# Fetching a GpSimd unit's blocks in the middle of the unit before it, and preparing chunks nine slots ahead, in a one-core RWKV-7 + FFN kernel

## The chip, the cores and the metric

One Trainium2 chip, one core of it. The metric is device time of one execution in microseconds (us). A result is the median of several executions. The kernel before took 1062.97 us (three runs, 1060.01 to 1065.29) when the prediction was made. For a program on one core the state of a run (fast or slow) is told from its distance to the fastest run of the same kernel.

## The reference

A recurrence over 768 steps for 4 batches and 8 heads of width 40, then a feed-forward block on its output. The kernel must give the (3072, 320) result.

```python
def _attn_ref(r, k, v, w, a, b):              # each (4, 8, 768, 40)
    for t in range(S):
        y[:, :, t] = einsum('bhd,bhde->bhe', r_t, state)
        Sa = einsum('bhde,bhe->bhd', state, a_t)
        state = state * w_t[:, :, None, :] - einsum('bhd,bhe->bhde', Sa, b_t) \
                + einsum('bhd,bhe->bhde', v_t, k_t)

x = y.transpose(0, 2, 1, 3).reshape(3072, 320)
h = maximum(x @ w_in, 0)                      # w_in (320, 2048)
out = (h * h) @ w_out                         # w_out (2048, 320)
```

## The kernel before

The sequence is cut into 24 chunks of 128 steps (6 for each of 4 batches). Within a chunk the recurrence becomes triangular systems of 64x64 blocks, two for each head. The work on a chunk has four parts: `prepare` makes the blocks N and stores them to HBM (`kept_d`, and decays to `kept_e`); GpSimd fetches them, solves the triangular systems, and stores the inverses (`kept_t`); `rest` loads the inverse T of the *next* chunk and makes its remaining operands; `chain` applies the chunk to the state. The feed-forward block (`second`) fills TensorE in between.

The loop goes over slots; slot i runs the chain of chunk i. GpSimd solves for several chunks at once, called a unit here: units 4 to 9 hold chunks 6-7, 8-9, 10-13, 14-17, 18-21 and 22-23. One unit must be stored before the next is fetched into the same tile `half_n`.

```python
def take(u, queues):                          # fetch the blocks of unit u
    ...
    for col in range(cols):
        queues[col % len(queues)].dma_start(out=part_of(u)[col * rows:(col + 1) * rows], in_=kept)

def solve(u, between={}):
    ...
    for s in range(size - 1):                 # 63 steps of two instructions
        if s in between:
            between[s]()
        ...
        nc.gpsimd.tensor_tensor(p_, part[...], t3[...], Alu.mult)
        nc.gpsimd.tensor_tensor(t3[...], t3[...], p_, Alu.subtract)
    ...
    nc.gpsimd.dma_start(out=to, in_=ts)       # the inverses, to kept_t
```

Apart from GpSimd's own fetches and stores and a few early transfers, loads and stores go through SyncE's one queue, in program order. A store is put off by a few steps; `flush` puts all that still wait into the queue. A load of a chunk's inputs:

```python
def load(i, g=None):
    x_ = loaded[i] = {"k": fetch("k", k, i)}
    if g is not None:
        ...
        nc.sync.dma_start(out=g["dec"][:USED], in_=kept_e[i])
    x_["r"] = fetch("r", r, i)
    later(lambda: x_.update(v=fetch("v", v, i), b=fetch("b", b, i)), ...)
```

And the loop. `ahead[i]` are the chunks prepared in slot i; `weave` interleaves the jobs of a slot; a unit is fetched and solved after the first slot that completes the preparation of its chunks.

```python
ahead = {0: (4, 5), 1: (6, 7), 2: (8,), 3: (9,), 4: (10, 11), 5: (12, 13)}
ahead.update({i: (i + 8,) for i in range(6, len(order) - 8)})
...
for i in range(len(order)):
    ...
    jobs = [(chain(i, g), 11, 0, TOTAL) if i else (first_slot, 10, 0, TOTAL)]
    jobs.append((some(second, n), n, begin, TOTAL))
    made = ahead.get(i, ())
    for j, m_ in enumerate(made):
        jobs.append((prepare(m_), 5, ...))
    done.update(made)
    if i + 1 < len(order):
        if i:
            ready[i + 1] = {}
            load(i + 1, ready[i + 1])
        jobs.append((rest(i + 1, ready[i + 1]), 9, 2, TOTAL))
    ...
    weave(*jobs)
    while unit < len(units) and all(m_ in done for m_ in ... if unit_of[m_] == unit):
        flush()
        take(unit, own)                       # own = [nc.gpsimd]
        solve(unit)
        unit += 1
```

## Time and profile before

| | before |
|---|---|
| median of 4 runs, beside the changed kernel | 1064.13 us (1060.01 to 1065.83) |
| span of the profiled execution | 1062.7 us |
| busy TensorE | 946.3 us (89%) |
| busy GpSimd | 667.7 us (63%) |
| mean granted TensorE clock | 0.900 |
| GpSimd's waits for stored blocks before a fetch | 36.3 us |

How to read it: the granted clock is the share of TensorE's full speed that it was allowed; half clock is 0.50. TensorE is the busiest engine, and slot 13 shows it full, with 0.3 us idle in 43.8 at clock 1.00; so a slot that is much longer than its like has either idle TensorE time or a clock below 1.00 in it. A line of SyncE's queue (SPq) tells when a transfer was issued and how long the issuing took, not when it landed. The token copies in it gather the recurrence's output for the feed-forward block. The lines themselves stand in the prediction.

### The profile page before, as it was taken

The page shows a single profiled execution, that of the slowest core. Times are in us where ns is not written, and L with a number is a line of the kernel's source. Part 1 is how long each engine was busy: PE and PEld are TensorE (multiplying, and loading weights), DVE is VectorE, ACT ScalarE, POOL GpSimd, SP SyncE. Part 2 cuts the span into 40 slices and gives each one's busy share as a digit, 9 for nine tenths or more (in the row PEclk, how much of TensorE's full clock was granted, in tenths as well). Part 3 has the DMA queues.
Part 4 walks back from the last instruction along what each step waited for, and adds up shares of the span by engine and source line. Part 5 has one row for each costly group of instructions (what it writes and reads, how often), then busy time and mean ns, then how long its engine had stood idle before and what let it go on. Part 6 is the DMA issues. An engine that isn't in the chain of part 4 may idle for free.

```text
span 1062.7 us, 19797 instructions
## 1 busy us (share of the span) xinstructions
PE 946.3 (89%) x7824; PEld 687.5 (65%) x7824; DVE 493.5 (46%) x940; ACT 273.3 (26%) x627; POOL 667.7 (63%) x1124
## 2 busy tenths in 40 slices
PE   6366667789999999997999998999997999999998
PEld 5255566576677766774677666776675677757656
DVE  5447786687463475442653453353522442222120
ACT  3132332343322223222212222213211222232020
POOL 4778464884888599981899951899968980000000
PEclk8656565568999999998999999899998999999999
DMA  8987989659457917447747618544345431430000
GB/s 109 149 142 141 183 185 184 138 123 195 87 90 127 196 32 115 89 64 171 113 60 135 112 55 148 91 97 77 50 112 95 65 48 53 97 46 7 22 1 19
DMA packets 260168, 106.92 MB, mean 101 GB/s; under 512 B 243660, under 2 KB 249292, under 8 KB 258412
## 3 DMA queue, kind: packets, MB, share of 16 engines
q1 hardware_dynamic: 255740, 86.65, 46.8%
q0 software_dynamic: 3248, 18.88, 7.7%
q8 instruction: 62, 1.02, 0.4%
q10 hardware_dynamic: 1088, 0.13, 0.1%
q14 instruction: 30, 0.25, 0.1%
HBM read 72.47 MB, written 31.19 MB: 98 GB/s over the span
## 4 chain that ended last, share of the span: by engine, by line
PE 60%; DMA 14%; POOL 13%; SPq 4%; DVE 3%; issue 3%; ACT 3%; POOLq 0%; ACTq 0%; DVEq 0%
PE ps_f L87 27%; PE ps_w L87 14%; PE ps_c L87 13%; POOL half_t L437 6%; POOL half_p L435 6%; DMA in_v<-in_v_dram 5%; PE ps_w L314 4%; SPq L108 2%; DMA in_k<-in_k_dram 2%; DMA half_n<-kept_d 1%; DMA tokens<-tokens 1%; DMA kept_t<-half_t 1%; DMA kept_e<-decay 1%; SPq L142 1%; PE ps_c L609 1%
## 5 line engine op out<-in xcount | busy, mean ns | idle before, releaser
L435 POOL TENSOR_TENSOR half_p<-half_n,half_t 128x70 f32<-128x70 f32 (+52 forms) x502 | 297.7, 593 | 111.3 <-DMA half_n<-kept_d 60.0
L437 POOL TENSOR_TENSOR half_t<-half_t,half_p 128x70 f32<-128x70 f32 (+52 forms) x502 | 322.6, 643 | 39.3
L87 PE MATMUL ps_f<-w_out,hid 128*128 128x320 f32 x672 | 202.0, 445 | 0.0
L87 PE MATMUL ps_f<-tokens,w_in 128*128 128x384 f32 x448 | 160.1, 500 | 0.0
L653 DVE TENSOR_TENSOR hid<-hid 128x384 f32<-128x384 f32 x128 | 91.8, 734 | 142.4 <-ACT hid L671 142.2
L87 PEld LDWEIGHTS ps_f<-w_out,hid 128*128 128x128 f32 x672 | 123.3, 193 | 46.7 <-issue 4.7
L87 PEld LDWEIGHTS ps_f<-tokens,w_in 128*128 128x128 f32 x448 | 80.8, 190 | 76.4 <-issue 32.1
L671 ACT ACTIVATE hid<-ps_f 128x384 f32<-128x384 f32 x112 | 54.9, 490 | 199.1 <-PE ps_f L87 199.1
L330 DVE TENSOR_TENSOR A<-ps_w,upper 128x512 f32<-128x512 f32 x48 | 30.9, 685 | 91.3 <-PE ps_w L87 91.3
L506 DVE TENSOR_TENSOR kvT<-ps_w,dec 128x512 f32<-128x512 f32 x24 | 16.5, 687 | 100.8 <-PE ps_w L314 60.8
L87 PE MATMUL ps_c<-xr,T 64*64 64x40 f32 x768 | 40.0, 245 | 21.3 <-DMA T<-kept_t 14.6
L87 PE MATMUL ps_f<-tokens,w_third 64*128 64x384 f32 x224 | 55.1, 540 | 0.0
L87 PEld LDWEIGHTS ps_c<-xr,T 64*64 64x64 f32 x768 | 33.3, 151 | 32.7 <-issue 16.0
L351 DVE TENSOR_TENSOR_SCAN decay<-ps_w,ones 128x64 f32<-128x64 f32 x88 | 23.6, 268 | 64.9 <-PE ps_w L314 64.8
L87 PE MATMUL ps_w<-decay,bT 40*128 40x128 f32 x352 | 30.9, 324 | 21.5 <-DVE decay L360 21.5
L87 PEld LDWEIGHTS ps_w<-decay,bT 40*128 40x128 f32 x352 | 26.1, 222 | 30.1 <-DVE decay L360 14.8
L330 DVE TENSOR_TENSOR RX<-ps_w,upper 128x512 f32<-128x512 f32 x48 | 30.8, 684 | 31.7 <-PE ps_w L87 31.5
L330 DVE TENSOR_TENSOR RV<-ps_w,upper 128x512 f32<-128x512 f32 x48 | 30.9, 685 | 21.9 <-PE ps_w L87 21.6
L87 PE MATMUL ps_w<-rT,xnT 40*128 40x128 f32 x384 | 37.1, 306 | 2.3 <-ACT rT L516 1.9
L355 DVE RECIPROCAL decay<-decay 128x256 f32<-128x256 f32 x22 | 38.3, 1740 | 0.0
L356 DVE RECIPROCAL decay<-decay 128x256 f32<-128x256 f32 x22 | 37.2, 1692 | 0.0
L87 PEld LDWEIGHTS ps_w<-rT,kvT 40*128 40x128 f32 x384 | 28.0, 209 | 13.2 <-issue 4.6
(139 smaller groups left out, 1401.7 us busy)
## 6 DMA issues: line engine op xcount, KB each, us to landing
kept_e<-decay SPq DMA_DIRECT2D x22, 633.8 KB
dec<-kept_e SPq DMA_DIRECT2D x22, 633.8 KB
hid<-in_moe_w_out_dram SPq DMA_DIRECT2D x16, 320.0 KB
half_n<-kept_d POOLq DMA_DIRECT2D x12, 384.0 KB, 11.2
half_n<-kept_d POOLq DMA_DIRECT2D x6, 768.0 KB, 12.0
in_w<-in_w_dram SPq DMA_DIRECT2D x24, 160.0 KB
in_ab<-in_b_dram SPq DMA_DIRECT2D x24, 160.0 KB
in_ab<-in_a_dram SPq DMA_DIRECT2D x24, 160.0 KB
```

What stands on the lines that cost most here:

```text
L87: nc.tensor.matmul(o, l_, r_, start=start, stop=True, skip_group_check=True)
L108: later(lambda: queue.dma_start(out=out_, in_=in_), steps)
L314: nc.tensor.transpose(p_[:, q * 128:(q + 1) * 128], pair(x_, q), ident)
L330: nc.vector.tensor_tensor(t_, p_, over4(upper), Alu.mult)
L351: nc.vector.tensor_tensor_scan(up[:, q, MID + 1:C + 1], wT[:, q, MID:], ones, 1.0, Alu.mult, Alu.mult)
L355: nc.vector.reciprocal(down[:, :, MID + 1:C + 1], up[:, :, MID + 1:C + 1])
L356: nc.vector.reciprocal(up[:, :, :MID], down[:, :, :MID])
L435: nc.gpsimd.tensor_tensor(p_, part[:, at:at + m_].unsqueeze(1).to_broadcast([128, n, m_]), t3[:, :n, s:s + 1].to_broadcast([128, n, m_]), ...
L437: nc.gpsimd.tensor_tensor(t3[:, :n, s + 1:], t3[:, :n, s + 1:], p_, Alu.subtract)
L506: nc.vector.tensor_tensor(kT, kT_, down[:, :, 1:C + 1], Alu.mult)
L653: nc.vector.tensor_tensor(h_, h_, h_, Alu.mult)
L671: nc.scalar.activation(h_, p_, Act.Relu)
```

## The change

The intent is to let GpSimd start its units earlier, so that T is there when TensorE comes to it. Four things are done. Unit 4 stops after 33 of its 63 steps to fetch the first two thirds of unit 5's blocks. To have these in time, chunks 8 and 9 are both prepared in slot 2. From slot 9 on preparation runs nine slots ahead, not eight (slot 9 prepares two chunks). And the two groups of small matmuls that join the halves of the fine units' inverses (units 0 to 3, which solve blocks of 32x32) alternate between the upper and lower partitions.

```diff
+    EARLIER = Q * HC
-    def take(u, queues):
+    def take(u, queues, words=slice(None)):
 ...
-            queues[col % len(queues)].dma_start(out=part_of(u)[col * rows:(col + 1) * rows], in_=kept)
+            queues[col % len(queues)].dma_start(out=part_of(u)[col * rows:(col + 1) * rows, words], in_=kept[:, words])
+    def solving(u, between={}, stop=None):      # solve(), as a generator
 ...
+            if s == stop:
+                yield
 ...
-        for one, two in ends_:
-            for h in range(H):
+        for h in range(H):
+            for one, two in ends_:
                 mm(p_[two, h], g["joins"][one, h], upper_[one, h], True)
 ... (the second group likewise)
-    ahead = {0: (4, 5), 1: (6, 7), 2: (8,), 3: (9,), 4: (10, 11), 5: (12, 13)}
-    ahead.update({i: (i + 8,) for i in range(6, len(order) - 8)})
+    ahead = {0: (4, 5), 1: (6, 7), 2: (8, 9), 3: (10,), 4: (11,), 5: (12, 13)}
+    ahead.update({i: (i + 8,) for i in range(6, 9)})
+    ahead[9] = (17, 18)
+    ahead.update({i: (i + 9,) for i in range(10, len(order) - 9)})
 ...
+    AHEAD, under_way = (FINE,), []              # FINE is 4
 ...
-            take(unit, own)
-            solve(unit)
+            if under_way:
+                take(unit, own, slice(0, EARLIER))
+                run(under_way.pop())
+                take(unit, own, slice(EARLIER, Q * (HC + Q)))
+            else:
+                take(unit, own)
+            if unit in AHEAD:
+                under_way.append(solving(unit, stop=Q + 1))
+                next(under_way[0])
+            else:
+                solve(unit)
```

More of the change, by code (lines that the diff above doesn't have):

```diff
@@ L411, in take @@
         for col in range(cols):
-            queues[col % len(queues)].dma_start(out=part_of(u)[col * rows:(col + 1) * rows], in_=kept)
+            queues[col % len(queues)].dma_start(out=part_of(u)[col * rows:(col + 1) * rows, words], in_=kept[:, words])
     def solve(u, between={}):
+        run(solving(u, between))
+    def solving(u, between={}, stop=None):
         first, nb = units[u]
@@ L483, in inverses @@
         p_ = small()
-        for one, two in ends_:
-            for h in range(H):
+        for h in range(H):
+            for one, two in ends_:
                 mm(p_[one, h], mv[two, h], blocks[two, h], True)
```

## The prediction

> **What bounds the kernel now.** I number the loop's steps as slots (slot i runs the chain of chunk i) and GpSimd's blocks of triangular solves as units: unit 4 solves chunks 6-7, unit 5 8-9, unit 6 10-13, unit 7 14-17, unit 8 18-21, unit 9 22-23. I read the page's slices first.
>
> ```profile
> PE   6366667789999999997999998999997999999998
> PEclk8656565568999999998999999899998999999999
> ```
>
> Until about slice 9 (some 240 us) TensorE is neither full nor at full clock: slots 0 to 3 run on latency and transfers. After that it is full, with dips. I then cut the span at slot starts (the matmuls into ps_c from A and in_v begin a slot): us, then busy us of PE, PEld, DVE, ACT, POOL, then granted clock, DMA share and GB/s. These are slots 1, 2, 4, 10, 13, 14, 18.
>
> ```profile
> 105.00:154.70 49.70, 33.06 (x332) 28.47 (x330) 38.02 (x69) 17.22 (x37) 28.05 (x80) 0.60 0.97 190
> 154.70:195.40 40.70, 31.31 (x293) 26.58 (x292) 26.83 (x57) 13.72 (x33) 21.98 (x49) 0.54 0.76 141
> 234.40:282.70 48.30, 45.35 (x410) 32.53 (x408) 34.47 (x73) 18.29 (x43) 31.99 (x75) 0.89 0.72 139
> 473.40:527.40 54.00, 45.50 (x342) 29.34 (x340) 23.20 (x43) 13.46 (x30) 27.47 (x47) 0.94 0.70 133
> 598.50:642.30 43.80, 43.48 (x342) 28.41 (x340) 21.33 (x44) 13.36 (x30) 27.02 (x38) 1.00 0.45 91
> 642.30:683.00 40.70, 37.31 (x316) 28.03 (x314) 14.17 (x30) 7.18 (x17) 20.56 (x35) 0.92 0.70 109
> 791.30:836.00 44.70, 37.18 (x297) 25.88 (x296) 11.98 (x22) 8.21 (x19) 32.83 (x62) 0.92 0.61 110
> ```
>
> Slot 13 is the healthy pattern: 0.3 us idle, clock 1.00. Slots 10, 14 and 18 lose idle time, and then clock: 6% of 54.0 = 3.2 us, 8% of 40.7 = 3.3, 8% of 44.7 = 3.6. TensorE's timeline says what each waits for.
>
> ```profile
> 487.09 1.08 PE L87 MATMUL ps_c<-xr,T 64*64 64x40 f32 x16 [7.07 <-DMA T<-kept_t]
> 663.76 0.63 PE L314 MATMUL ps_w<-ident,in_r 128*128 128x128 f32 x4 [2.88 <-DMA in_r<-in_r_dram]
> 803.75 1.08 PE L87 MATMUL ps_c<-xr,T 64*64 64x40 f32 x16 [7.52 <-DMA T<-kept_t]
> ```
>
> So TensorE's work is the bound from 240 us on, plus three interruptions. GpSimd's own timeline says where they come from (start, duration, then the wait before).
>
> ```profile
> 250.62 0.60 POOL L440 DMA_DIRECT2D kept_t<-half_t  x1 [0.30 <-POOL half_t L437]
> 255.83 0.96 POOL L425 MEMSET half_t<- 128x1024 f32 x1 [2.67 <-DMA kept_t<-half_t]
> 265.67 0.28 POOL L435 TENSOR_TENSOR half_p<-half_n,half_t 128x63 f32<-128x63 f32 x1 [8.23 <-DMA half_n<-kept_d]
> ...
> 479.40 0.60 POOL L440 DMA_DIRECT2D kept_t<-half_t  x1 [0.30 <-POOL half_t L437]
> 490.35 1.03 POOL L412 DMA_DIRECT2D half_n<-kept_d  x2 [10.35 <-DMA kept_d<-N]
> ...
> 647.25 1.03 POOL L412 DMA_DIRECT2D half_n<-kept_d  x2 [18.62 <-DMA kept_d<-N]
> ...
> 784.52 0.60 POOL L440 DMA_DIRECT2D kept_t<-half_t  x1 [0.30 <-POOL half_t L437]
> 798.76 0.29 POOL L435 TENSOR_TENSOR half_p<-half_n,half_t 128x63 f32<-128x63 f32 x1 [7.21 <-DMA half_n<-kept_d]
> ```
>
> The stall at 487 is unit 6 ending late (479.40): true GpSimd lateness. The one at 663 is unit 8's 1.5 MB fetch, issued at 647.25, burying the loads of slot 14. The one at 803 looks like GpSimd, but is not: unit 8 was stored at 784.5; the SyncE queue shows the load of T behind token copies, which lie under unit 9's fetch.
>
> ```profile
> 786.82 13.33 SPq L108 DMA_DIRECT2D tokens<-tokens  x8
> 800.25 1.37 SPq L451 DMA_DIRECT2D T<-kept_t  x2
> ```
>
> **What the Trainium skill says.** "DMA: Bandwidth & Descriptors", Queues, rings and completion order: each DMA engine takes turns between its queues, packet by packet. The trace agrees: half_n moves in 12 KB rows, T in 256 B rows, tokens in 1.5 KB rows, so small rows beside a fetch get a turn per big row, and the token copies ended (800.2) only as the fetch did (798.8). "TensorE: Matmul & The Clock Gate", What's actually happening: an idle window of about 3.4 us halves the clock. The trace agrees after both 7 us stalls (xr,T takes 1.08 us, 0.66 elsewhere); a wait of 2.88 + 0.43 us (in_r, in_v) was enough in slot 14. "TensorEngine Tiling (Array Packing)", Key Properties: different tiles can run in parallel. Only in part here: matmuls of 40x128 on alternating halves take 72 ns each (1.16 us / 16)[...], but the 64x40 ones, which alternate already, take 41 ns, no less than that rule gives (37).
>
> **The change, part by part.** (a) *Fetch within unit 4.* It stops after step 32 (about 214.8 us in the old trace) to issue four fetches of the first 2/3 of unit 5's words (4 x 0.49 = 2.0 us), and the last third after its end. Its end moves from 250.6 to 252.6. Unit 5 now waits only for unit 4's store (5.2 us, as 250.62 to 255.83) and two kinds of memset (1.6): it starts at 259.4 instead of 265.7, 6.3 us earlier. Needed: chunk 9's first blocks by 214.8. Both 8 and 9 are made in slot 2 now; slot 2, with two preparations, should grow from 41 towards slot 1's 50 us, ending about 202, and stores end some 8 to 12 us later: just in time, 0 to 3 us of wait possible. (b) *Units 5 and 6* then run 79.8 us, 12.5 of fetch and 121.3 us: unit 6 ends at 473.1, not 479.4. (c) *Slot 9 prepares 17 and 18*: 2.9 us of TensorE work (transposes 0.6 + 1.1, products 1.16) comes ahead of the first stall, so TensorE comes to chunk 10's T at about 483, not 480. Free of other traffic T would arrive 7.7 us after unit 6's end (as 479.40 to 487.09), at 480.8, and the stall would vanish. But the stores of chunk 17 now go into the SyncE queue *before* the load of T (they came behind it, which made unit 7 wait until 490.35). So unit 7's fetch leaves at once and meets T's load. By unit 9's case (784.52 to 798.76) it takes 14.2 us from a unit's end: 487.3, and T comes about 1 us after it, 488. Gain there: 2.9 us of work done early, less 0.9 of later T: 2.0 us, the clock loss staying. (d) *Unit 7* starts at 487.5 instead of 506.3, ends at 609.3 (121.8 us). Its fetch no longer falls on slot 10's in_r and in_v (1.2 us of stall), but they queue behind the late T: net 0 to 1. (e) *Nine ahead*: chunk 21 is made in slot 12, so unit 8 starts fetching at 609 rather than 647, in the middle of slot 13, when its loads are done. Slot 14's stall goes: 3.3 + 3.3 of clock = 6.6 us. Unit 8 ends at 609.3 + 14.2 + 121.2 = 744.7; unit 9's fetch then ends near 759, long before slot 17's token copies. They take about 6 us (188.25 to 194.6 in the same trace), T comes 7 us sooner: 7.5 + 3.6 of clock, less 0.5 left over, 10.6 us. (f) *Early slots*: slot 2 grows by some 7, slot 4 shrinks by some 4 to 6 (one preparation less). Unless TensorE comes to chunk 10 after 488, it hides in the wait for T. (g) *Joins*: 32 matmuls of 54 ns at half clock (34 at full), twice in each of six chunks. With 41 ns for those that alternate already I expect at most 0.3 us a group, under 2 us of busy time, in slots that wait for transfers: 0. Sum: 2.0 + 0.5 + 6.6 + 10.6 = 19.7, less 1 for a new collision around 745 to 760 (slot 17's loads of in_k and dec): 18.7. 1063 - 19 = **1044 us**.
>
> **Rivals.** (1) *T does not meet the fetch, or passes it.* Then the whole 7.07 goes with its 3.2 of clock, 6 to 9 us more: 1036. For: T is only 256 KB; against: the token copies at 787. (2) *Unit 4 waits in its middle for chunk 9.* Early DMA is nearly full (0.97 in slot 1) and half clock rules there; each us of that wait moves units 5, 6 and T: 1049 if 5 us. For: the estimate is just in time. (3) *The fetches only collide elsewhere*: unit 9's with slot 17, unit 5's 1 MB at 215 with slot 3. If slot 17 stalls as slot 14 did, 6.6 comes back: 1050. Against: slot 17's in_k was asked 7.5 us before its slot. (4) *The early slots grow beyond what the wait hides* (slot 2 past 52): 1 us for 1 us, 1050 to 1056.
>
> **Range and chances.** 1034 to 1055: rival 1 sets the low end, two of the others together the high one. 2% faster is 1041.7, just under my figure: faster 0.38, within 2% 0.59, slower 0.03. Most of the gain rests on two stalls whose cause is seen in the trace, hence little chance of slower.
>
> **What would show it.** Unit 5's first solve about 6 us earlier; half_n's waits for kept_d (36.3 us in all) below 12; unit 6's end at 471 to 476, T's matmul at 486 to 490 after a wait of 3 to 6; no waits of 2 us for in_r nor for T in slots 14 and 18; clock 1.00 there; busy PE nearly unchanged (946), its idle some 15 us less. Wrong would be: T on time at 481 (rival 1); unit 4's middle waiting over 4 us (2); a new TensorE wait of over 2 us in slots 15 to 17 (3); slot 5 starting over 8 us later (4).

## The result, and the profile after

The changed kernel took 1051.36 us (median of four runs, 1047.30 to 1053.37), the kernel before 1064.13 us in the same rounds: a ratio of 0.9881, 95% interval 0.9837 to 0.9925. Ratios here are always the mean time of one kernel's fast runs over the mean of the other's fast runs of the same rounds, so not quite the ratio of the quoted medians. The gain is 1.2%, 12.8 us by the medians: within 2%, and inside the range. It is less than the 19 us that the prediction's sum had.

The profiled execution of the changed kernel spans 1045.6 us. It is the fastest of the four runs (1047.30 us as timed), while the profiled execution of the kernel before (1064.37 us as timed) lies at its median; so part of the 17.1 us between the two profiles is the draw of the execution.

The page's slices of the changed kernel, to be held against the first two lines of the prediction:

```profile
PE   6364665688999999997999999999999999999998
PEclk8656676667999999998999999999999999999999
```

After slice 9 one dip is left where there were three. It is the one that the prediction said would stay, around 480 us. The same cut at slot starts, for slots 2, 10, 14, 15 and 18 of the changed kernel (us, busy us of PE, PEld, DVE, ACT, POOL, granted clock, DMA share, GB/s):

```profile
152.80:202.80 50.00, 31.24 (x323) 27.05 (x320) 32.46 (x69) 15.46 (x37) 29.70 (x61) 0.64 0.87 170
477.50:528.40 50.90, 45.22 (x344) 29.43 (x343) 26.40 (x43) 13.36 (x30) 38.80 (x49) 0.93 0.74 144
643.30:677.40 34.10, 33.78 (x316) 25.92 (x314) 15.79 (x30) 7.08 (x17) 31.67 (x32) 1.00 0.33 60
677.40:712.70 35.30, 33.83 (x296) 24.04 (x294) 11.92 (x20) 8.92 (x21) 33.02 (x30) 1.00 0.70 125
783.40:819.00 35.60, 35.06 (x299) 24.47 (x298) 12.10 (x22) 8.21 (x19) 31.92 (x48) 1.00 0.62 109
```

Slots 14 and 18 are healthy: 0.3 and 0.5 us idle, clock 1.00; they are 6.6 and 9.1 us shorter in this cut. Slot 10 still has 5.7 us of idle time and clock 0.93. TensorE's timeline shows the two waits that are left:

```profile
489.53 1.08 PE L87 MATMUL ps_c<-xr,T 64*64 64x40 f32 x16 [5.44 <-DMA T<-kept_t]
687.36 0.66 PE L314 MATMUL ps_w<-ident,in_k 128*128 128x128 f32 x4 [0.96 <-DMA in_k<-in_k_dram]
```

T at 489.53 came 2.4 us *later* than before (487.09), although GpSimd was earlier. The wait of 0.96 us for in_k in slot 15 is new. GpSimd's timeline of the changed kernel (start, duration, wait before):

```profile
213.44 2.00 POOL L415 DMA_DIRECT2D half_n<-kept_d  x4
258.15 0.29 POOL L443 TENSOR_TENSOR half_p<-half_n,half_t 128x63 f32<-128x63 f32 x1
488.18 0.28 POOL L443 TENSOR_TENSOR half_p<-half_n,half_t 128x63 f32<-128x63 f32 x1 [6.11 <-DMA half_n<-kept_d]
610.52 1.03 POOL L415 DMA_DIRECT2D half_n<-kept_d  x2 [0.16 <-DMA dec<-kept_e]
```

The fetch in the middle of unit 4 left at 213.44 without a wait, and unit 5 began to solve at 258.15, 7.5 us earlier than before. Unit 7 began at 488.18, and T was taken 1.35 us after that. Unit 8's fetch left at 610.52, not 647.25. GpSimd's waits for blocks that were not yet stored, from the view of waits (total us, times, longest), were 36.3 us before:

```profile
POOL half_n L415 <- DMA kept_d<-N: 7.3, 1, 7.3
```

SyncE's queue at the end of slot 17 and the start of slot 18 answers to the last two lines of the prediction's first part. The eight token copies took 6.32 us in place of 13.33, and the load of T went out in time:

```profile
778.88 6.32 SPq L108 DMA_DIRECT2D tokens<-tokens  x8
785.30 1.38 SPq L459 DMA_DIRECT2D T<-kept_t  x2
```

Where the 17.1 us of this pair of profiles lie: slot 10 ended 0.9 us later (528.35 against 527.45), slot 14 gave 6.5, slot 15 gave 2.4 (the preparation that slot 9 now does, less the new wait), slot 18 gave 9.2. That is 17.2.

### The profile page after: what moved, and what is told of

Its sections match the earlier page's. It is cut to its first block, busy times and chain, and to the rows that moved or that the text cites.

```text
span 1045.6 us, 19803 instructions
## 1 busy us (share of the span) xinstructions
PE 927.4 (89%) x7824; PEld 672.1 (64%) x7824; DVE 496.8 (48%) x940; ACT 273.0 (26%) x627; POOL 670.6 (64%) x1128
## 4 chain that ended last, share of the span: by engine, by line
PE 52%; POOL 28%; DMA 10%; issue 5%; DVE 2%; ACT 2%; SPq 1%; POOLq 0%; DVEq 0%; ACTq 0%
PE ps_f L87 26%; POOL half_t L445 14%; POOL half_p L443 13%; PE ps_w L87 11%; PE ps_c L87 10%; DMA half_n<-kept_d 3%; PE ps_w L314 2%; DMA kept_t<-half_t 1%; DMA half_n<-kept_q 1%; DMA in_w<-in_w_dram 1%; DMA T<-kept_t 1%; DMA w_out<-in_moe_w_in_dram 1%; PE ps_w L542 1%; DMA kept_m<-N 1%; POOL half_n L415 1%
## 5 line engine op out<-in xcount | busy, mean ns | idle before, releaser
L443 POOL TENSOR_TENSOR half_p<-half_n,half_t 128x70 f32<-128x70 f32 (+52 forms) x502 | 298.9, 595 | 90.2 <-DMA half_n<-kept_d 39.8
L87 PE MATMUL ps_f<-w_out,hid 128*128 128x320 f32 x672 | 198.6, 440 | 0.0
L87 PE MATMUL ps_f<-tokens,w_in 128*128 128x384 f32 x448 | 162.3, 506 | 0.0
L661 DVE TENSOR_TENSOR hid<-hid 128x384 f32<-128x384 f32 x128 | 94.4, 752 | 139.4 <-ACT hid L679 139.0
L87 PEld LDWEIGHTS ps_f<-w_out,hid 128*128 128x128 f32 x672 | 121.6, 190 | 44.9 <-issue 2.1
L514 DVE TENSOR_TENSOR kvT<-ps_w,dec 128x512 f32<-128x512 f32 x24 | 16.5, 687 | 88.7 <-DMA dec<-kept_e 46.6
L87 PE MATMUL ps_c<-xr,T 64*64 64x40 f32 x768 | 39.1, 242 | 13.7 <-ACT xr L592 6.7
L351 DVE TENSOR_TENSOR_SCAN decay<-ps_w,ones 128x64 f32<-128x64 f32 x88 | 23.8, 270 | 54.2 <-PE ps_w L314 54.1
L87 PEld LDWEIGHTS ps_c<-xr,T 64*64 64x64 f32 x768 | 32.5, 148 | 25.1 <-ACT xr L592 13.1
L87 PE MATMUL ps_w<-rT,xnT 40*128 40x128 f32 x384 | 34.2, 293 | 2.4 <-ACT rT L524 2.4
L524 ACT COPY rT<-ps_w 128x512 f32<-128x512 f32 x24 | 14.0, 585 | 82.5 <-PE ps_w L314 82.5
```

The lines of the kernel that those rows point to most:

```text
L87: nc.tensor.matmul(o, l_, r_, start=start, stop=True, skip_group_check=True)
L351: nc.vector.tensor_tensor_scan(up[:, q, MID + 1:C + 1], wT[:, q, MID:], ones, 1.0, Alu.mult, Alu.mult)
L443: nc.gpsimd.tensor_tensor(p_, part[:, at:at + m_].unsqueeze(1).to_broadcast([128, n, m_]), t3[:, :n, s:s + 1].to_broadcast([128, n, m_]), ...
L514: nc.vector.tensor_tensor(kT, kT_, down[:, :, 1:C + 1], Alu.mult)
L524: nc.scalar.copy(rT, turn(x_["r"]))
L661: nc.vector.tensor_tensor(h_, h_, h_, Alu.mult)
```

## The experiments

Twelve kernels ran (one of them the changed kernel again), all gave correct results, in three batches of four. Each batch was on one chip and shared its runs of the kernel before (medians 1065.53, 1063.97, 1063.76 us). Slot lengths are from each kernel's one profile.

| kernel | median us | ratio to before (95%) | slot 10 | slot 14 | slot 15 | slot 18 |
|---|---|---|---|---|---|---|
| before | 1064.13 | 1 | 54.1 | 40.6 | 37.7 | 44.7 |
| changed | 1051.36 | 0.9881 (.9837-.9925) | 50.9 | 34.1 | 35.3 | 35.6 |
| *batch 1:* after_again | 1050.90 | 0.9858 (.9831-.9886) | 49.8 | 34.4 | 39.8 | 35.7 |
| t_first | 1053.68 | 0.9886 (.9863-.9908) | 57.5 | 34.1 | 35.1 | 35.6 |
| no_mid_fetch | 1053.39 | 0.9889 (.9867-.9911) | 53.0 | 34.1 | 35.2 | 35.6 |
| no_nine | 1063.89 | 0.9988 (.9963-1.0013) | 50.3 | 41.1 | 37.4 | 44.9 |
| *batch 2:* k_first | 1049.10 | 0.9851 (.9828-.9874) | 53.2 | 34.3 | 34.5 | 35.6 |
| t_k_first | 1041.37 | 0.9789 (.9770-.9809) | 43.8 | 34.1 | 34.5 | 35.6 |
| r_first | 1041.91 | 0.9785 (.9765-.9805) | 44.9 | 34.1 | 34.5 | 35.6 |
| only_nine | 1051.43 | 0.9885 (.9864-.9906) | 52.8 | 34.1 | 35.4 | 35.6 |
| *batch 3:* before_late9 | 1063.73 | 1.0007 (.9981-1.0033) | 49.9 | 40.3 | 37.4 | 40.1 |
| old_joins | 1050.17 | 0.9875 (.9850-.9899) | 49.9 | 34.4 | 37.0 | 35.9 |
| t_k_no_mid | 1043.73 | 0.9814 (.9790-.9837) | 45.0 | 34.1 | 34.5 | 35.6 |
| nine_late | 1068.81 | 1.0059 (1.0027-1.0091) | 72.6 | 34.1 | 35.7 | 35.7 |

The theory under test: nearly all of the gain is the nine-ahead order, which takes big fetches off the loads of slots 14 and 18; in slot 10 the earlier GpSimd is worth little because unit 7's fetch now meets the load of T. The rivals: the mid-unit fetch carries the gain; GpSimd is simply still late in slot 10; the joins matter.

### after_again: the changed kernel, unchanged

> The changed kernel unaltered, a second time: how far its executions spread, and whether its profile is the same in the places that count. Theory (mine, from the two profiles): slot 10 waits 5 to 6 us for the T of chunk 10, slots 14 and 18 wait for nothing; 1047 to 1054 us. Rival: the profile of the changed kernel was a lucky execution (it is the fastest of four), and others show a further wait of 3 us or more, which explains why the median gain is 12 us where the profile's is 17.

Measured: 1050.90 us, ratio 0.9858, profiled span 1051.5 us. This profile is nearer the median than the first one, and it shows a loss that the first did not. The first line is slot 15 of it from the cut by windows, the second its start of work on in_k:

```profile
678.70:718.50 39.80, 36.86 (x294) 25.86 (x292) 12.53 (x20) 8.92 (x21) 37.21 (x34) 0.91 0.63 111
```

```profile
690.12 1.11 PE L314 MATMUL ps_w<-ident,in_k 128*128 128x128 f32 x4 [2.43 <-DMA in_k<-in_k_dram]
```

The wait for in_k was 2.43 us here, and the matmuls after it ran at half clock (1.11 us for what took 0.66); the slot lost 4.5 us against the first profile. SyncE's queue shows why the wait exists at all. First the kernel before, whose slot 15 began at 682.95; then this one, whose slot 15 began at 678.66:

```profile
685.34 0.40 SPq L142 DMA_DIRECT2D in_k<-in_k_dram  x1
...
688.77 3.57 SPq L108 DMA_DIRECT2D kept_d<-N  x4
```

```profile
680.04 4.49 SPq L108 DMA_DIRECT2D kept_d<-N  x4
...
685.28 0.56 SPq L142 DMA_DIRECT2D in_k<-in_k_dram  x1
```

Before, the load of in_k went out 2.4 us into the slot, ahead of the stores of prepared blocks; now these stores come first and it goes out 6.6 us into the slot. What follows: the changed kernel has one new wait, in slot 15, which cost about 1 us in one profile and about 5 in the other (39.8 us against the 34.5 that the slot takes without it, in k_first below). Both profiles have the same order in the queue; what differs is how long the load took to land after its issue (3.3 and 4.8 us) and the clock after it. Seven kept profiles have this order: in five of them slot 15 took 35.1 to 35.7 us, in old_joins 37.0 and here 39.8, so the dear case is seen in two of seven. The expectation missed in slot 10: TensorE waited 3.02 us for T, not 5 to 6. It came 1.8 us later to it than in the first profile, T came 0.7 earlier, and the slot ended at 529.01 (528.35 there).

### no_nine and only_nine: the order of preparation, taken out and alone

no_nine is the changed kernel with `ahead` from slot 6 on as before:

```diff
-    ahead.update({i: (i + 8,) for i in range(6, 9)})
-    ahead[9] = (17, 18)
-    ahead.update({i: (i + 9,) for i in range(10, len(order) - 9)})
+    ahead.update({i: (i + 8,) for i in range(6, len(order) - 8)})
```

> The changed kernel with the old look-ahead of eight slots from slot 9 on. Theory: the stores of chunk 17 come again behind the load of T, unit 7's fetch leaves after T has landed, T comes at about 483, the wait in slot 10 shrinks to 1 to 2 us without half clock; but unit 8's fetch falls on slot 14's loads again (6 to 7 us lost there) and unit 9's on the token copies before slot 18 (3 to 8 us lost). Sum: 3 to 8 us over the changed kernel, 4 to 10 under the kernel before. Rival (nine ahead does nothing but fill slot 10): slots 14 and 18 without waits.

only_nine is the kernel before with these lines alone:

```diff
-    ahead.update({i: (i + 8,) for i in range(6, len(order) - 8)})
+    ahead.update({i: (i + 8,) for i in range(6, 9)})
+    ahead[9] = (17, 18)
+    ahead.update({i: (i + 9,) for i in range(10, len(order) - 9)})
```

> The kernel before with the nine slots ahead from slot 9 on, and nothing else of the change. Theory: early slots as before (4 us shorter than in the changed kernel); unit 6 ends at 479 to 480, unit 7's fetch leaves at once, T comes with its end at about 494, TensorE comes there at 483: about 10 us of wait. Slots 14 and 18 lose nothing. 2 to 6 us over the changed kernel, 1053 to 1056. Rival (the early parts of chunks 8 and 9 and the fetch in unit 4 only pay for each other): equal to the changed kernel, 1050 to 1052.

Measured: no_nine 0.9988, not told apart from the kernel before. That is some 13 us over the changed kernel (1063.89 and 1050.90), where 3 to 8 had been expected: a miss in size. only_nine 0.9885, not told apart from the changed kernel (0.9881, 0.9858): the 2 to 6 us over it did not show, and by time the rival written down came true. In no_nine both stalls are back; TensorE's timeline in slot 14, then SyncE's queue before slot 18's T:

```profile
665.95 0.63 PE L314 MATMUL ps_w<-ident,in_r 128*128 128x128 f32 x4 [3.94 <-DMA in_r<-in_r_dram]
```

```profile
788.20 13.16 SPq L108 DMA_DIRECT2D tokens<-tokens  x8
```

What follows: the nine-ahead order carries nearly all of the gain. The mid-unit fetch, the early parts and the joins together are worth 0.4 to 3 us by these ratios; the intervals allow more. That the fetch alone makes in_r late in slot 14 has no run of its own: the new order also issues that load earlier (640.93, before slot 14, in place of 647.28, 5 us into it). The late issue alone hardly explains the wait, since in the kernel before in_r was issued 13.6 us before TensorE came to it and landed 16.5 us after its issue, but this rival was not tested. One thing more is to be seen in no_nine: its fetch of unit 7 had to wait until 488.15, so T travelled without it and was taken at 484.96, 8.5 us after unit 6's end (476.44), after a wait of 0.62 us only. In only_nine unit 6 ended at 477.18, the fetch left at once (477.94), and T was taken 14.7 us after the end, after a wait of 6.96 us. This speaks for the fetch as what makes T late in slot 10. Why no_nine gained nothing there all the same: it came to slot 10 at 477.73, 4.3 us later than the kernel before, waited 1.79 us for in_r, had a mean clock of 0.93, and ended the slot at 527.99 (527.45 before).

### no_mid_fetch: the changed kernel without the fetch in unit 4

```diff
-    AHEAD, under_way = (FINE,), []
+    AHEAD, under_way = (), []
```

> The changed kernel without the fetch in the middle of unit 4; all the rest stays. Theory (GpSimd's chain units 4-5-6 sets when T comes): unit 5 starts about 6 us later, unit 6 ends at 478 to 481 instead of 475, T's matmul comes that much later too; 3 to 6 us over the changed kernel, nearly all in slot 10. Rival (the gain comes from the schedule alone; the fetch is hidden): within 1.5 us of the changed kernel.

Measured: 0.9889 against 0.9858 in the same batch; the intervals overlap, so about 3 us that are not certain. Unit 5 began to solve at 264.42 after a wait of 7.49 us, unit 6 ended at 478.21 (475.06 in the changed kernel), and T was taken at 492.86. What follows: the mid-unit fetch moves unit 5 by 6.3 us, as foreseen, unit 6's end by 3.2, and T by 3.3, which is about what comes to the time. The last two are from one pair of profiles: in the eight kernels that have this fetch (nine_late left out) unit 6 ended between 473.2 and 477.9, in the three with the nine-ahead order and without the fetch between 476.7 and 478.2, so its end moves by 2.0 us on the mean.

### t_first, k_first, t_k_first, r_first: is the fetch what delays T in slot 10?

t_first makes GpSimd read one column of chunk 10's T before it issues unit 7's fetch, so that the two cannot meet. (Nothing uses the product.)

```diff
         flush()
+        if unit == 7:
+            first_t = ready[i + 1]["T"][:, 0, :1]
+            nc.gpsimd.tensor_tensor(new("half_p", [128, 528], 1)[:, :1], first_t, first_t, Alu.mult)
```

> GpSimd reads one value of chunk 10's T before it issues the fetch of unit 7, so that the fetch cannot be in flight while T is loaded. Theory (T comes late because the fetch takes the transfer engines): T lands 7.7 us after unit 6's end as in the kernel before, so about 483, TensorE comes there at 484 and does not wait; the 5.4 us wait and the half clock after it (some 3.3 us) go, less about 1 us of new waits for in_r and in_v in slot 10: 6 to 9 us under the changed kernel, the profile at 1037 to 1040. Rival (T is late because unit 6's own store or the SyncE queue is): T still lands 13 to 15 us after unit 6's end, no gain, or a loss of up to 1 us since unit 7 starts later.

Measured: 0.9886, no better than the changed kernel. This was a miss. Lines of TensorE's timeline, then of GpSimd's:

```profile
486.15 0.66 PE L87 MATMUL ps_c<-xr,T 64*64 64x40 f32 x16 [1.73 <-DMA T<-kept_t]
...
500.29 1.09 PE L314 MATMUL ps_w<-ident,in_k 128*128 128x128 f32 x4 [9.27 <-DMA in_k<-in_k_dram]
```

```profile
486.16 0.18 POOL L835 TENSOR_TENSOR half_p<-T 128x1 f32<-128x1 f32 x1 [7.69 <-DMA T<-kept_t]
```

The wait for T fell to 1.73 us, as it should: unit 6 ended at 477.87, and T landed 8.3 us later, not 14.5 as in the changed kernel. But a wait of 9.27 us for in_k took its place. In SyncE's queue the loads of the next chunk (in_k at 493.85) stand behind T and the stores, and now it was they that met the fetch. The collision had moved, not gone.

So k_first moves the load of a chunk's inputs one slot earlier, to the end of the slot before the one that used to issue it, behind T but ahead of the stores:

```diff
         if i + 1 < len(order):
-            if i:
-                ready[i + 1] = {}
-                load(i + 1, ready[i + 1])
             jobs.append((rest(i + 1, ready[i + 1]), 9, 2, TOTAL))
 ...
         weave(*jobs)
+        if i + 2 < len(order):
+            ready[i + 2] = {}
+            load(i + 2, ready[i + 2])
```

> The changed kernel, but the loads of k, dec and r for slot i are put into the SyncE queue at the end of slot i-2, ahead of the batch of stores that a finished unit flushes there (they came behind it). Theory (the second profile of the changed kernel loses 2.4 us and then half clock in slot 15, because k of chunk 16 is queued behind token copies and chunk 23's stores): that wait goes in every execution; 1 to 4 us under the changed kernel's 1051, and executions lie closer together. Slot 10 unchanged, T of chunk 10 with the end of unit 7's fetch. Rival (slot 15's wait comes from elsewhere): no change.

Measured: 0.9851, not told apart from the changed kernel; the 1 to 4 us foreseen are not shown. Slot 15 lost its new wait (34.5 us long, here and in the three other kernels with this edit), which confirms the cause found in after_again. Slot 10 took 2.4 to 3.5 us more than in the two profiles of the changed kernel: T was taken at 490.43 after a wait of 5.95 us, and the slot's mean clock was 0.90 (0.93 in the first of them).

t_k_first is both edits together:

> k_first with the gate of t_first: GpSimd reads one value of chunk 10's T before it issues unit 7's fetch. In t_first T came in time but k of chunk 11, queued behind stores, fell under the fetch instead (9.3 us). Theory: k now lies right behind T and N in the queue and lands by about 489 or soon after, needed at 491: waits of 0 to 2 us for it, 0 to 2 for in_r; 5 to 8 us under k_first, 1040 to 1044. Rival (any load of slot 10 that the fetch meets costs the same): a wait of over 5 us for k, N or dec, and no gain over k_first.

Measured: 1041.37 us, 0.9789, the interval clear of the changed kernel's (whether it is 2% faster than the kernel before stays unclear, as it reaches 0.9809). Slot 10 is 43.8 us long with the clock at 1.00, like the healthy slot 13. GpSimd's timeline, then TensorE's:

```profile
482.08 0.18 POOL L835 TENSOR_TENSOR half_p<-T 128x1 f32<-128x1 f32 x1 [7.12 <-DMA T<-kept_t]
482.75 1.06 POOL L415 DMA_DIRECT2D half_n<-kept_d  x2 [0.48 <-DMA N<-kept_n]
```

```profile
484.67 0.66 PE L87 MATMUL ps_c<-xr,T 64*64 64x40 f32 x16
489.48 0.66 PE L314 MATMUL ps_w<-ident,in_k 128*128 128x128 f32 x4
```

Unit 6 ended at 474.36, T landed 7.7 us later, before TensorE wanted it, and the fetch left after it. Neither T nor in_k is waited for. Against k_first, from which it differs by the gate alone, in the same batch, that is 7.7 us by the medians and 6.8 by the means.

r_first is k_first with the gate on in_r of chunk 11, whose load stands behind T's in SyncE's queue, in place of T:

```diff
+        if unit == 7:
+            seen = loaded[i + 2]["r"][:, 0, :1]
+            nc.gpsimd.tensor_tensor(new("half_p", [128, 528], 1)[:, :1], seen, seen, Alu.mult)
```

> k_first with the gate on r of chunk 11 instead of T of chunk 10: the fetch of unit 7 leaves only when T, N, k, dec and r have landed, about 490 to 494. Theory: no TensorE wait over 1 us in slot 10; unit 7 then starts at about 506, as in the kernel before, ends at 627, and unit 8's fetch runs 627 to 641, across the start of slot 14: there 0 to 4 us lost. 4 to 9 us under k_first. Rival (later unit 7 gives back as much in slot 14): equal to k_first.

Measured: 1041.91 us, 0.9785, the same as t_k_first, though its fetch left only at 490.53, 8 us later than there: unit 7 has that much to spare. What follows from the four: in slot 10 GpSimd's end was early enough in the changed kernel, or nearly so (with the later end of t_first, 477.87, a wait of 1.73 us was left), and the fetch on top of T's load cost what was left of the stall. Removing it pays only when the loads behind T are out of the fetch's way too. These two are the best versions found, 2.1% below the kernel before and 7 to 10 us below the changed one (0.9789 against 0.9858 and 0.9881).

### t_k_no_mid: t_k_first without the mid-unit fetch

```diff
-    AHEAD, under_way = (FINE,), []
+    AHEAD, under_way = (), []
```

> t_k_first without the fetch in the middle of unit 4. Theory: unit 6 ends 3 to 4 us later (478 instead of 474.4), T lands at 486, TensorE comes at 484: a wait of 1 to 4 us in slot 10, 1 to 4 us over t_k_first, more (5 to 7) if that wait halves the clock. So the early fetch still has a worth once the collision is gone. Rival: equal to t_k_first.

Measured: 1043.73 us, 0.9814; slot 10 took 45.0 us, 1.2 more than in t_k_first, with waits of 0.28 us for T (1 to 4 had been expected; unit 6 ended at 476.69, not 478) and 0.84 for in_v. Against 0.9789 (another batch, and the intervals touch) that is about 2.6 us, so the mid-unit fetch is worth some 2 to 3 us in either version, and neither comparison is certain by itself.

### nine_late: what an unready chunk 9 would cost

The changed kernel with chunk 9 prepared in slot 3 again, so that the fetch in the middle of unit 4 must wait for it:

```diff
-    ahead = {0: (4, 5), 1: (6, 7), 2: (8, 9), 3: (10,), 4: (11,), 5: (12, 13)}
+    ahead = {0: (4, 5), 1: (6, 7), 2: (8,), 3: (9,), 4: (10, 11), 5: (12, 13)}
```

> The changed kernel, but chunks 8 and 9 prepared in slots 2 and 3 as before, so that the fetch in the middle of unit 4 has to wait for chunk 9's blocks. Theory (rival 2 of the prediction, forced): GpSimd stands in unit 4 from about 214 until slot 3 ends and its stores land, some 238 to 242, 24 to 28 us; units 5 and 6 and the T of chunk 10 come about 18 to 22 us later than in the changed kernel, TensorE waits over 20 us in slot 10: 14 to 22 us over the changed kernel, slower than the kernel before. Rival (the early parts do not matter): within 3 us of the changed kernel.

Measured: 1068.81 us, some 18 us above the changed kernel and above the kernel before. GpSimd's timeline, then TensorE's:

```profile
232.24 2.00 POOL L415 DMA_DIRECT2D half_n<-kept_d  x4 [19.66 <-DMA kept_d<-N]
```

```profile
507.53 1.08 PE L87 MATMUL ps_c<-xr,T 64*64 64x40 f32 x16 [27.11 <-DMA T<-kept_t]
```

A wait of 19.66 us at 232 became 18.0 us of later T 275 us on (507.53 against 489.53). This is the prediction's rival 2 in the open, and it shows that the early parts are needed for the mid-unit fetch: GpSimd has no slack from there to slot 10.

### old_joins: the joins as before

```diff
-        for h in range(H):
-            for one, two in ends_:
+        for one, two in ends_:
+            for h in range(H):
```
(twice)

> The changed kernel with the joins in the old order (one pair of blocks after the other). Theory (their matmuls lie in slots that wait for transfers, and what they delay is hidden in the wait for chunk 10's T): a group of 32 takes 1.7 us at half clock again instead of 1.06 to 1.45, some 5 us more of busy TensorE in all, and the time stays within 1.5 us of the changed kernel (ratio 0.985 to 0.989). Rival (the joins stand on the path of the early slots and these on the path to the end): 3 to 5 us slower than the changed kernel.

Measured: 0.9875, between the two results of the changed kernel. The first group of 32 matmuls in one slot at half clock, the changed kernel's and then this one's:

```profile
149.12 1.06 PE L87 MATMUL ps_w<-hid 32*32 32x32 f32 x32
```

```profile
149.26 1.72 PE L87 MATMUL ps_w<-hid 32*32 32x32 f32 x32
```

The matmuls do get faster when they alternate; the second group there took 1.45 us against 1.73. By the groups of the whole profile the two groups took 19.4 us of busy TensorE here and 12.9 in the changed kernel. The slots that hold them wait for transfers, and no change of the time is seen.

### before_late9: is slot 18's stall unit 9's fetch alone?

The kernel before, with unit 9's fetch held back until slot 17, and there until T has landed:

```diff
     while unit < len(units) and ...:
+        if unit == 9 and i < 17:
+            break
         flush()
+        if unit == 9:
+            seen = ready[i + 1]["T"][:, 0, :1]
+            nc.gpsimd.tensor_tensor(new("half_p", [128, 528], 1)[:, :1], seen, seen, Alu.mult)
         take(unit, own)
```

> The kernel before, with unit 9 put off until slot 17 and its fetch sent only when T of chunk 18 has landed; nothing else. Theory (the 7.5 us wait in slot 18 is unit 9's fetch slowing the token copies ahead of T in the queue, not GpSimd's lateness): the eight token copies are issued in about 6 us instead of 13.3, T comes within 1 us of TensorE's need, no half clock after it: 8 to 11 us under the kernel before, ratio 0.990 to 0.993; unit 9 ends near 892, needed at about 925. Rival (T of chunk 18 is late because unit 8 ends late): the wait stays at over 5 us and the time does not change.

Measured: 1.0007, no gain, where 8 to 11 us had been expected: a miss in time. The mechanism is as thought; SyncE's queue, then TensorE's timeline:

```profile
789.36 6.53 SPq L108 DMA_DIRECT2D tokens<-tokens  x8
```

```profile
799.45 0.66 PE L87 MATMUL ps_c<-xr,T 64*64 64x40 f32 x16 [0.69 <-DMA T<-kept_t]
```

With the fetch away the token copies took 6.53 us, not 13.33, and the wait for T fell from 7.52 to 0.69. Slot 18 still took 40.1 us, because the held-back fetch now met the load of in_k (1.93 us of wait, then half clock): 4.7 us gained, not 9. Why even these do not appear in the median is not settled. This profile reached slot 10 at 480.12, 6.7 us later than that of the kernel before, with the same instructions up to there; so the early slots alone can scatter by that much between executions (2.6 us of it were left at slot 10's end, 530.05 against 527.45).

## Why the prediction was right, point by point

The class (within 2%) and the range held; the figure was 7 us too low. By its own steps:

- **(a) Fetch within unit 4: right.** Unit 5 was to start at 259.4 and started at 258.15. The fetch was to be just in time, with 0 to 3 us of wait, and had none. nine_late shows that the worry behind rival 2 was real in size, yet it did not come true.
- **(b) Unit 6's end: 2 us off.** Predicted 473.1, measured 475.06. Unit 5 ended at 338.81, as the sum has it (259.4 + 79.8 = 339.2), but then the fetch of unit 6 took 14.95 us until the first solve, not the 12.5 carried over from the old trace (13.5 to 16.1 in the eight profiles with the mid-unit fetch, 12.3 to 12.8 in the five without). Some 6.8 us earlier, it fell on slot 6's own loads (in_w and in_ab were still in SyncE's queue; one of them was 9.76 us there); in the old trace it had followed them. A duration of a transfer was taken along to another time without asking what lies beside it.
- **(c) T meets unit 7's fetch: right in mechanism, nearly right in size.** T was predicted at 488 and taken at 489.53, 1.35 us after the fetch had landed (predicted about 1). t_k_first, r_first and no_nine show that without the fetch T comes within 0.7 us of TensorE. That small rows get "a turn per big row" is an inference; no run shows single packets. The gain was put at 2.0 + 0.5; it was 2.3: the preparation done ahead gave 3.2 us in slot 15 (37.7 less the 34.5 without the new wait), less 0.9 of later end of slot 10. Of the two terms, T came 2.4 us later, not 0.9, and most of that was made up behind it in the slot.
- **(d) Unit 7: right, in part by luck.** Start 488.18 (predicted 487.5), end 609.76 (609.3). Unit 6 had ended 2.0 us later than said, and the fetch then took 13.1 us, not 14.2.
- **(e) Nine ahead: right in place and cause.** Slot 14 gave 6.5 (predicted 6.6). Slot 18 gave 9.2, not 10.6. Here the mis-sized term is the clock: its idle time fell by 7.0 us as predicted (7.5 less 0.5), but its busy time by 2.2 us only. The prediction turned the slot's mean clock straight into lost time (8% of 44.7 = 3.6). In slot 14, with 3.4 us idle, that was right (3.5 us less busy time); there the clock was 1.00 during the wait and fell after it. In slot 18, with 7.5 us idle, it fell during the wait (granted clock 0.71 from 800.0 to 803.7, TensorE idle), and slow clock in idle time costs nothing.
- **(f) Early slots: half right.** Slot 2 grew by 9.3 us to 50.0 (predicted some 7, ending about 202; it ended at 202.8). Slot 4 did not shrink by 4 to 6 but by 0.4; slot 3 shrank by 4.6 instead. The sum was only 2.4 us at the start of slot 5, and it lay under the wait for T as said. Since one and the same early code came to slot 5 at 282.7, 286.5 and 291.6 in three profiles (before, only_nine, before_late9), no more should be read from these sizes.
- **(g) Joins: too small, harmless.** "At most 0.3 us a group" was 0.66 us in the first group shown, and "under 2 us of busy time" was 5.8 (18.7 us in all before, 12.9 after). The 0.3 rested on matmuls of another shape. By the rate of 356 ns for 384 columns, 40 columns take an estimated 37 ns, and the 64x40 ones, which alternate already, took 41; that they gained nothing from alternating did not carry over to the 32x32 ones. Their effect on the time was to be 0 and was none that could be measured.
- **The new collision: wrong place, wrong size.** The 1 us set aside for slots 16 and 17 was not lost there. It was lost in slot 15, and not to a fetch: stores of prepared blocks came to stand before the load of in_k. It cost 0.8 us in one profile and, through the clock, 5.3 in the other. This is the largest piece between the profiles' 17 and the medians' 13 to 15 that was found; that it was dear in two of seven profiles is too little to say how much of the difference it makes.
- **What was to show it: one test was ill made.** "Busy PE nearly unchanged, its idle some 15 us less" came out otherwise: busy fell by 18.9 us (946.3 to 927.4) and idle rose by 1.8. The two parts of the span hide each other. Up to slot 5 busy fell by some 12 us (5.8 of it in the joins, the rest with a clock of 0.71 in place of 0.67, which after_again, the same kernel, did not have), and idle rose by 14, since these slots wait for transfers anyway. From slot 5 on idle fell by 12.3 and busy by some 7. The test should have been set on slots 5 and after.

Of the rivals, (1) was refuted as a description of this kernel, but its 6 to 9 us are what t_k_first gained over k_first by making it true; (2) did not occur; (3) occurred in small with unit 6's fetch in slot 6, without a loss of TensorE time there (34.5 us, 35.0 before); (4) did not come through to the time. The 7 us by which the figure was too low are 1.6 us of mis-sized terms (18.7 predicted, 17.1 between the profiles), 1.1 of a kernel before that ran at 1064.13 and not 1063, and 4.3 between the 17.1 and the medians' 12.8, since the fastest execution of the changed kernel was the profiled one.

## What to carry to other kernels

A large fetch can make the small loads beside it much later (T came 14 us after its unit's end in place of 8), so when a producer is made earlier, write down which small loads its next fetch will now meet, at its new time. Where one has to give way, hold the large one back until the small ones have landed (one read of the small tile on the engine that issues the fetch is enough), and see that *all* urgent loads are issued ahead of it, else the wait only changes its name. When a change has several parts, run each alone: here the order of preparation carried nearly the whole gain.

## What the Trainium skill lacked or had wrong

- "DMA: Bandwidth & Descriptors", Queues, rings and completion order, tells that each DMA engine takes turns between queues by packets. It has no figure for what this does to a small load beside a large one. Here chunk 10's T (256 B rows) was there 7.7 to 8.5 us after its unit's end when alone (six profiles) and 13.7 to 14.7 us after it beside a fetch in 12 KB rows (seven), and eight token copies took 6.3 to 6.5 us alone and 13.2 to 13.3 beside one.
- "TensorE: Matmul & The Clock Gate", What's actually happening, gives an idle window of about 3.4 us for the fall to half clock. Shorter idle time was followed by it here. In slot 15 of after_again one wait of 2.43 us, in a slot with 2.94 us of idle time in all, was (1.11 us for four transposes in place of 0.66). In slot 15 of old_joins a wait of 1.01 us was, some 2 us later (granted clock 0.50 from 690 to 692 us). Waits of 0.76 to 1.39 us at the same place in five other profiles were not, so the length of the wait alone did not decide. For planning, waits of 1 to 3 us have to be counted as able to halve the clock; the two slots took 5.3 and 2.5 us more than the 34.5 without the wait, over twice the wait each.
- "TensorEngine Tiling (Array Packing)", Key Properties, says that different tiles can run in parallel. No page has a figure for what the order of issue does to that. The same 32 matmuls of 32x32 took 1.72 us when issued one partition half after the other and 1.06 us when issued in turns, both at half clock.
